# Where four pieces of work stand in a local-attention and mixture-of-experts kernel: slot 0's weights, its table, the first value sums, the query reorders

## The chip, the core and the metric

The kernel runs on one NeuronCore of a Trainium2 chip, as one launch. The metric is the device time of one execution in microseconds (us), lower is better. TensorE is PE in the profile (its weight loads PEld), VectorE DVE, ScalarE ACT, GpSimd POOL, SyncE SP. All loads of inputs and weights are issued from SP's queue in an order that the program fixes; POOL issues the stores of intermediate rows, the gathers and the scatters.

## The reference

The inputs are q, k, v of shape (4, 8, 768, 64): 4 batches, 8 heads, 768 positions, head size 64. Attention is local (a key counts where its position is less than 16 away) plus 24 summary keys per head, one for each block of 32 positions. The result, 3072 tokens of 512 numbers, goes through a mixture of 8 experts, one expert for each token.

```python
k_sum = k.reshape(B, H, nb, 32, D).max(axis=3)
v_sum = v.reshape(B, H, nb, 32, D).mean(axis=3)
scores_l = where(|pos_q - pos_k| < 16, q @ k.T / 8, -1e9)
scores_s = q @ k_sum.T / 8 + log(32)
a = softmax(concat([scores_l, scores_s]))
x = a @ concat([v, v_sum])                      # as (3072, 512)
logits = x @ w_gate;  e = argmax(logits, axis=1)
weight = softmax(logits)[e] * sigmoid(x @ w_output_gate)[e]
out = weight * (relu(x @ w1[e]) @ w2[e])        # w1[e]: 512 x 1024, w2[e]: 1024 x 512
```

## The kernel before

**Attention.** `attention` walks over 48 stages: 4 batches (b), 6 tiles of 128 tokens in each (tok), 2 halves of 4 heads (g). A stage is `scores` (PE multiplies queries `qt` with keys `kt` into `sp`; DVE adds the mask and takes the row's minimum into `sm`, `mn`; ACT takes the exponential into `pr`), `turn_p` (PE transposes `pr` into `pt`, copied to `pT`) and `values` (PE multiplies `pT` with the values `vw` into `pv`; DVE divides by the sum into `xs`). In names of buffers the digits are batch, tile, half: `sm301` is batch 3, tile 0, half 1. `todo` and `second` hang smaller work onto the stages: gate logits, routing, the preparation of the next keys and queries.

**Queries and keys.** Three loads per batch, u = 0 to 2, bring 256 positions each into `raw_q` and `raw_k`. `reorder` copies them into `nat_q` and `nat_k`, mostly on DVE; `prep_q` and `prep_k` transpose those on PE into `qt` and `kt`. `prep_k` also takes the maxima `km` on DVE, and `k_sum` copies `km` into `kt` (four copies, one for each pair of heads). The query load of two u ahead is issued at the first tile of a u, and its reorder stands right behind the load in the program:

```python
            if n2 and tt == 0:
                load("q", q, *n2)
                reorder("q", *n2, RE[5])
```

**Value sums.** `load_vm` brings the values of four heads into `vm` (o = 0 and 1), `v_sum` adds up each block of 32, `mean` divides and stores into the DRAM buffer `vs_dr`, and `load_vsum` brings that into the `vw` tiles. In batch 0 both sums are on DVE (`tensor_reduce`, two halves each); in later batches GpSimd adds them in five halving steps (96x1024, 512, 256, 128, 64).

**The experts.** After two batches the router's counts give a table of three early slots of 256 tokens (`early_slots`, at the event "routed", after stage 36: batch 3, tile 0). `Experts.start` then hangs slot 0's work onto the tiles of batch 3 (`late_work[tok]`): `fetch_list` (which tokens), `fetch` (gathers their rows into `xg`), and `fetch_w` for 12 weight pieces of 256 KB, three on each of the tiles 1 to 4. Every piece is a load on SP into `raw` (6 buffers), a rounding on ACT (`w1h`, `w2h`) and a remainder on DVE (`w1l`, `w2l`). `fetch_w` first has SP read the slot's expert number from the table. `Experts.early` and the slots behind it run once attention has ended.

**What sets the order.** SP's order is that of the program. On PE, DVE, ACT and (in attention) POOL a scheduler that works with modelled times sets the order when the program is built, starting from the order in which the program names the work; on the chip each engine then runs its list strictly in order.

Of the kernel before, what the change touches and what calls it, by code (L numbers as in the profile page):

```python
# [14 lines left out]
AF = mybir.ActivationFunctionType  # L15
ALU = mybir.AluOpType
AX = mybir.AxisListType
# [4 lines left out]
P = 128  # L22
HP = H // 2
NB = S // 64
# [78 lines left out]
def body(tc, q, k, v, w_gate, w_ogate, w1, w2, ident, cst, out):  # L103
    nc = tc.nc
    with (
        tc.tile_pool(name="const", bufs=1, side="left") as const,
        tc.tile_pool(name="ps", bufs=2, space=PSUM) as ps,
        tc.tile_pool(name="dr", bufs=1, space=DRAM) as dr,
        tc.tile_pool(name="tail", bufs=1, side="right") as st,
    ):  # L110
        id_sb = const.tile([P, P], F32, name="id_sb")
        nc.sync.dma_start(id_sb, ident)
        c_sb = const.tile([P, C_END], F32, name="c_sb")
        nc.gpsimd.dma_start(c_sb, cst)
        wg_sb = const.tile([P, NC, 32], F32, name="wg_sb")
        nc.gpsimd.memset(wg_sb, 0.0)
        nc.gpsimd.dma_start(wg_sb[:, :, 0:E], w_gate.rearrange("(c p) e -> p c e", p=P))
        nc.gpsimd.dma_start(wg_sb[:, :, E:2 * E], w_ogate.rearrange("(c p) e -> p c e", p=P))
        x_dr = dr.tile([N, DM], F32, name="x_dr")
        l_dr = dr.tile([E * N + P, 2], I32, name="l_dr")  # L120

        pool_a = tc.tile_pool(name="early", bufs=1, side="left")
        pool_b = tc.tile_pool(name="late", bufs=1, side="right")
        sa, sb = pool_a.__enter__(), pool_b.__enter__()
        rt = route_setup(tc, const, sa, ps, c_sb, l_dr)
        moe = Experts(tc, const, ps, w1, w2, id_sb, x_dr, l_dr, rt, out)
        late_work = [[] for _ in range(TB)]
        with tc.manual_schedule(engines={mybir.EngineType.SP}):
            for event in attention(tc, const, sa, sb, st, ps, dr, q, k, v, id_sb, c_sb, wg_sb, x_dr, l_dr, rt, late_work):
                if event == "last batch":  # L130
                    pool_a.__exit__(None, None, None)
                    moe.open_first(tc.tile_pool(name="moe1", bufs=2, side="left", reuse_waits="tile"))
                elif event == "routed":
                    moe.add_slots(early_slots(tc, const, c_sb, rt))
                    moe.start(late_work)
                elif event[0] == "tiles done":
                    with tc.manual_schedule(engines={mybir.EngineType.Pool}):
                        moe.early(event[1])
        pool_b.__exit__(None, None, None)
        moe.open_second(tc.tile_pool(name="moe2", bufs=2, side="right", reuse_waits="tile"))  # L140
        with tc.manual_schedule(engines={mybir.EngineType.Pool}):
            with tc.manual_schedule(engines={mybir.EngineType.DVE}):
                moe.fetch_w(2, ("e", 0), range(NF // 2, NF))
                moe.fetch_w(1, ("e", 1), range(NF // 2))
            moe.fetch_w(1, ("e", 1), range(NF // 2, NF))
            moe.second(("e", 0), 2, *moe.hidden0, ("e", 1), ("e", 2), 2, 2)
            counts = rest_slots(tc, const, c_sb, rt, moe)
            moe.run()
        moe.rest(counts)
        moe.close()  # L150
# [27 lines left out]
def attention(tc, const, sa, sb, st, ps, dr, q, k, v, id_sb, c_sb, wg_sb, x_dr, l_dr, rt, late_work):  # L178
# [53 lines left out]

    def v_sum(b, o, half):
        t = vm[b, o]
        if b == 0:
            if half == 0:
                vs[b, o] = sb.tile([96, D], F32, name=f"vs{b}{o}", tag="vs", bufs=2)
            hs = slice(32 * half, 32 * half + 32)
            nc.vector.tensor_reduce(out=vs[b, o][:, hs], in_=t.rearrange("p (s d) -> p d s", d=D)[:, hs, :], axis=AX.X, op=ALU.add)
            if half == 1:  # L240
                mean(b, o, vs[b, o])
            return

        n = 16 * D
        if half == 0:
            nc.gpsimd.tensor_tensor(t[:, 0:n], t[:, 0:n], t[:, n:2 * n], ALU.add)
            return
        while n > D:
            n //= 2
            nc.gpsimd.tensor_tensor(t[:, 0:n], t[:, 0:n], t[:, n:2 * n], ALU.add)  # L250
        mean(b, o, t[:, 0:D])

    def mean(b, o, total):
        r2 = sb.tile([96, D], F32, name=f"vm2{b}{o}", tag="vs2", bufs=2)
        nc.vector.tensor_scalar(r2, total, 1.0 / 32.0, None, ALU.mult)
        nc.gpsimd.dma_start(vs_dr[b, 4 * o:4 * o + 4].rearrange("g n d -> (g n) d"), r2)

    def load_vw(b, tok):
# [42 lines left out]
    def k_sum(b):  # L301
        kt = KT[b % 2]
        for hp in range(HP):
            own = kt[:, hp, PAD:PAD + NB * KW].rearrange("p (i w) -> p i w", w=KW)[:, :, 32:56]
            nc.vector.tensor_copy(own, km[b, 0][:, hp, :].unsqueeze(1).to_broadcast([P, NB, NS]))  # L305

    def prep_q(b, u, gs=(0, 1)):
        qt = QT[(3 * b + u) % 2]
# [204 lines left out]
    for i, (b, tok, g) in enumerate(stages):  # L513
        u, tt = tok // 2, tok % 2
        n1, n2 = step_after(b, u), step_after(b, u, 2)
        more = b + 1 < B
        if (b, tok, g) == (B - 1, 0, 0):
            yield "last batch"
        if g == 0:
            if n2 and tt == 0:  # L520
                load("q", q, *n2)
                reorder("q", *n2, RE[5])
            load_ahead(*((b + 1, tok) if tok < 4 else (b + 2, tok - 6)))
            if more and tok in (0, 1, 3):
                reorder("k", b + 1, (tok + 1) // 2, RE[6])
            if (tok + 2 < TB or more) and (b, tok) != (0, 0):
                nb, ntok = divmod(b * TB + tok + 2, TB)
                load_vw(nb, ntok)
                load_vsum(nb, ntok)
        first, second = todo.pop(i, []), []  # L530
        s = 2 * tt + g
        if n1 and s == 0:
            first.append(lambda: prep_q(*n1, gs=(0,)))
        if n1 and s == 1:
            second.append(lambda: prep_q(*n1, gs=(1,)))
        if more and s == 0:
            second.append(lambda: prep_k(b + 1, u, (0,)))
        if more and s == 2:
            second.append(lambda: prep_k(b + 1, u, (1,)))
            if u == 2:  # L540
                second.append(lambda: k_sum(b + 1))
        if more and u < 2 and s in (1, 3):
            second.append(lambda: v_sum(b + 1, u, s // 2))
        if b == B - 1:
            w = late_work[tok]
            take = w[:-(-len(w) // 2)] if g == 0 else w[:]
            del w[:len(take)]
            second += take
        if i + 1 < n:
            scores(i + 1)  # L550
        for work in first[:1]:
            work()
        turn_p(i)
        second = first[1:] + second
        for work in second:
            work()
        if i > 0:
            values(i - 1)
            pb, ptok, pg = stages[i - 1]
            if pg == 1:  # L560
                todo.setdefault(i + 1, []).append(lambda pb=pb, ptok=ptok: turn_x(pb, ptok))
                if ptok % 2 == 1:
                    todo.setdefault(i + 2, []).append(lambda pb=pb, ptok=ptok: logits(pb, ptok))
                    todo.setdefault(i + 4, []).append(lambda pb=pb, ptok=ptok: turn_logits(pb, ptok))
                if ptok == TB - 1:
                    todo.setdefault(i + 4, []).append(lambda pb=pb: route_to(pb))
                    todo.setdefault(i + 6, []).append(lambda pb=pb: route_to(pb))
        if i == n - 2 * TB:
            yield "routed"
    for i in sorted(todo):  # L570
        for work in todo[i]:
# [154 lines left out]
class Experts:  # L726
# [38 lines left out]
    def fetch_list(self, s, n):  # L765

        nc, tc = self.tc.nc, self.tc
        nm = f"lst_{s[0]}{s[1]}"
        lst = self.const.tile([P, 2, 2], I32, name=nm, tag=nm)
        for t in range(n):  # L770
            i = nc.gpsimd.indirect_dma_start(out=lst[:, t, :], out_offset=None, in_=self.l_dr,
                                             in_offset=bass.IndirectOffsetOnAxis(ap=self.slots[s][0][t], axis=0))
# [82 lines left out]

    def start(self, late_work):

        self.fetch_list(("e", 0), 2)
        late_work[1] += [lambda: self.fetch(("e", 0), 2)]
        late_work[3] += [lambda: self.fetch_list(("e", 1), 2)]  # L860
        parts = [(1, i) for i in range(NF)] + [(2, i) for i in range(NF // 2)]
        for x, (which, i) in enumerate(parts):
            late_work[1 + x * 4 // len(parts)].append(lambda which=which, i=i: self.fetch_w(which, ("e", 0), [i]))

    def early(self, route):

# [180 lines left out]
```

## Time and profile before

| | |
|---|---|
| median of 3 runs | 545.28 us (544.25, 545.28, 550.03) |
| profiled execution | 543.33 us, of which the span from the first to the last instruction is 541.5 us |
| PE busy | 494.3 us (91%), mean granted clock 0.964 |
| DVE busy | 395.6 us (73%) |
| ACT busy | 336.9 us (62%) |
| POOL busy | 200.0 us (37%) |
| moved by DMA | 117.98 MB, mean 218 GB/s |

Times in the profile count from the span's start. A row of the timeline gives start, length, engine, line, operation and tiles, and in brackets how long the engine stood idle before it and what ended that. SPq and POOLq rows are DMA issues, whose length is the issue and not the transfer. A line number belongs to the kernel before.

### The profile page before, as it was taken

The page shows a single profiled execution, that of the slowest core. Times are in us where ns is not written, and L with a number is a line of the kernel's source. Part 1 is how long each engine was busy: PE and PEld are TensorE (multiplying, and loading weights), DVE is VectorE, ACT ScalarE, POOL GpSimd, SP SyncE. Part 2 cuts the span into 40 slices and gives each one's busy share as a digit, 9 for nine tenths or more (in the row PEclk, how much of TensorE's full clock was granted, in tenths as well). Part 3 has the DMA queues.
Part 4 walks back from the last instruction along what each step waited for, and adds up shares of the span by engine and source line. Part 5 has one row for each costly group of instructions (what it writes and reads, how often), then busy time and mean ns, then how long its engine had stood idle before and what let it go on. Part 6 is the DMA issues. An engine that isn't in the chain of part 4 may idle for free.

```text
span 541.5 us, 12266 instructions
## 1 busy us (share of the span) xinstructions
PE 494.3 (91%) x3880; PEld 431.7 (80%) x3880; DVE 395.6 (73%) x1242; ACT 336.9 (62%) x752; POOL 200.0 (37%) x225
## 2 busy tenths in 40 slices
PE   6499998989878899999999999999999999999990
PEld 6497787777767688899898988989897887886970
DVE  7979798769938878989657657665767866767770
ACT  4487786586748957465556546555556756658560
POOL 7037155545451252343734160511332421511421
PEclk7699998999979999999999999999999999999995
DMA  8979899899783757695947658495576795597641
GB/s 247 236 199 269 212 233 282 158 201 235 169 202 79 264 172 235 238 240 129 351 160 264 204 206 291 142 307 172 202 248 218 271 334 193 208 324 235 207 149 30
DMA packets 117052, 117.98 MB, mean 218 GB/s; under 512 B 53787, under 2 KB 78651, under 8 KB 116192
## 3 DMA queue, kind: packets, MB, share of 16 engines
q1 hardware_dynamic: 107584, 97.02, 63.2%
q0 software_dynamic: 9376, 19.91, 11.6%
q8 instruction: 36, 0.59, 0.5%
q14 instruction: 56, 0.46, 0.3%
HBM read 106.30 MB, written 13.79 MB: 222 GB/s over the span
## 4 chain that ended last, share of the span: by engine, by line
PE 66%; DMA 12%; DVE 7%; ACT 5%; issue 5%; POOL 2%; SPq 1%; POOLq 0%; ACTq 0%; DVEq 0%
PE yp L935 8%; PE hp L836 8%; PE hp L835 8%; PE yp L933 8%; PE yp L934 8%; PE hp L837 8%; PE sp L330 6%; DMA xg<-x_dr,lst_w 5%; DMA raw_q<-in_q_dram 3%; PE pv L359 3%; PE pt L348 2%; PE xp L817 2%; ACT pr L340 2%; DMA vm<-in_v_dram 2%; ACT qt L201 1%
## 5 line engine op out<-in xcount | busy, mean ns | idle before, releaser
L836 PE MATMUL hp<-xhl,w1h 128*128 128x256 f32 x384 | 108.8, 284 | 0.3 <-issue 0.3
L835 PE MATMUL hp<-xhl,w1h 128*128 128x256 f32 x384 | 108.5, 284 | 0.3 <-PE yp L935 0.3
L837 PE MATMUL hp<-xhl,w1l 128*128 128x256 f32 x384 | 108.5, 283 | 0.0
L933 PE MATMUL yp<-w2h,hh 128*128 128x512 f32 x216 | 86.7, 401 | 1.3 <-ACT hh L904 1.2
L935 PE MATMUL yp<-w2h,hl 128*128 128x512 f32 x216 | 85.0, 396 | 0.2
L934 PE MATMUL yp<-w2l,hh 128*128 128x512 f32 x216 | 84.9, 393 | 0.0
L340 ACT ACTIVATE pr<-sm,mn 128x120 f32<-128x120 f32 x192 | 62.0, 387 | 23.5 <-DVE mn L338 22.5
L784 POOL DMA_INDIRECT xg<-x_dr,lst_w x26 | 30.2, 1162 | 125.2 <-PE xp L817 120.2
L835 PEld LDWEIGHTS hp<-xhl,w1h 128*128 128x128 f32 x384 | 73.2, 191 | 2.4 <-issue 1.2
L836 PEld LDWEIGHTS hp<-xhl,w1h 128*128 128x128 f32 x384 | 73.5, 191 | 2.0 <-issue 1.0
L837 PEld LDWEIGHTS hp<-xhl,w1l 128*128 128x128 f32 x384 | 73.5, 191 | 0.0
L838 ACT ACTIVATE hh<-hp 128x256 fp32r<-128x256 f32 x96 | 35.3, 380 | 52.8 <-PE hp L837 43.8
L839 DVE SCALAR_TENSOR_TENSOR hl<-hp,hh 128x256 fp32r<-128x256 f32 x96 | 39.0, 420 | 39.3 <-ACT hh L838 25.3
L330 PE MATMUL sp<-kt,qt 128*128 128x120 f32 x384 | 57.7, 298 | 7.0 <-DVE kt L305 6.0
L330 PEld LDWEIGHTS sp<-kt,qt 128*128 128x128 f32 x384 | 52.7, 211 | 10.0 <-issue 7.7
L338 DVE CUSTOM_DVE_ANT_0 sm<-sp,c_sb 128x120 f32<-128x120 f32 x192 | 42.9, 276 | 15.1 <-PE sp L330 9.3
L933 PEld LDWEIGHTS yp<-w2h,hh 128*128 128x128 f32 x216 | 40.7, 188 | 10.2 <-ACT hh L904 2.1
L935 PEld LDWEIGHTS yp<-w2h,hl 128*128 128x128 f32 x216 | 40.4, 188 | 9.7 <-DVE hl L905 1.2
L934 PEld LDWEIGHTS yp<-w2l,hh 128*128 128x128 f32 x216 | 40.7, 188 | 7.8
L348 PE MATMUL pt<-id_sb,pr 128*120 128x128 f32 x192 | 38.9, 290 | 2.9 <-ACT pr L340 2.9
L359 PE MATMUL pv<-vw,pT 120*64 120x65 f32 x768 | 34.9, 228 | 3.3 <-DMA raw_('e', 0)_6_2972<-in_moe_w_dram 1.6
L359 PEld LDWEIGHTS pv<-vw,pT 120*64 120x64 f32 x768 | 27.8, 137 | 11.7 <-issue 3.9
(735 smaller groups left out, 1043.4 us busy)
## 6 DMA issues: line engine op xcount, KB each, us to landing
vw<-in_v_dram SPq DMA_DIRECT2D x88, 96.0 KB
raw_k<-in_k_dram SPq DMA_DIRECT2D x12, 512.0 KB
raw_q<-in_q_dram SPq DMA_DIRECT2D x12, 512.0 KB
vm<-in_v_dram SPq DMA_DIRECT2D x8, 768.0 KB
x_dr<-xs POOLq DMA_DIRECT2D x24, 256.0 KB
vw<-vs_dr SPq DMA_DIRECT2D x36, 48.0 KB
vw<-in_v_dram SPq DMA_DIRECT2D x8, 64.0 KB
xg<-x_dr,lst_w POOLq DMA_INDIRECT x26
```

The costliest lines, as they stand in the source:

```text
L330: nc.tensor.matmul(sp[:, 2 * x + y, 0:W], lhsT=qt[:, 2 * g + x, li, :], rhs=kt[:, 2 * g + x, blk * KW:blk * KW + W], start=True, stop=True)
L338: nc.vector.tensor_tensor_reduce(out=sm[:, c, :], in0=sp[:, c, 0:W], in1=c_sb[:, m:m + W], scale=1.0, scalar=3.0e38, op0=ALU.add, op1=ALU. ...
L340: nc.scalar.activation(pr[:, c, :], sm[:, c, :], AF.Exp, bias=mn[:, c:c + 1], scale=-1.0)
L348: nc.tensor.transpose(pt[:, c, :], pr[:, c, :], id_sb)
L359: nc.tensor.matmul(po[64 * y:64 * y + 64, 2 * x + hh, :], lhsT=pT[:, 2 * x + y, 64 * hh:64 * hh + 64], rhs=VW[(NB * b + 2 * tok + y) % VR] ...
L835: nc.tensor.matmul(hp, lhsT=w_h[:, fs], rhs=self.xh[:, c, :], start=c == 0, stop=False)
L836: nc.tensor.matmul(hp, lhsT=w_h[:, fs], rhs=self.xl[:, c, :], start=False, stop=False)
L837: nc.tensor.matmul(hp, lhsT=w_l[:, fs], rhs=self.xh[:, c, :], start=False, stop=c == NC - 1)
L839: nc.vector.scalar_tensor_tensor(hl[:, j, :], hp, 0.0, hh[:, j, :].bitcast(F32), ALU.max, ALU.subtract)
L933: nc.tensor.matmul(y, lhsT=hh[:, j, tk], rhs=w_h, start=j == 0, stop=False)
L934: nc.tensor.matmul(y, lhsT=hh[:, j, tk], rhs=w_l, start=False, stop=False)
L935: nc.tensor.matmul(y, lhsT=hl[:, j, tk], rhs=w_h, start=False, stop=j == NF - 1)
```

## The change

Five edits. (1) `Experts.start` is called at "last batch", before stage 36, and its lists move: the weight pieces to tiles 0 to 3, three each; slot 0's list to tile 1 and its gather to tile 2. (2) The event "routed", with the early slots' table, comes after stage 33 (batch 2, tile 4). (3) In batch 0 the sum o = 1 takes the GpSimd way of the later batches and its mean is a GpSimd instruction; the sum o = 0 stays on DVE, but may not be scheduled ahead of the last `k_sum` copy, and its mean goes to ACT. (4) The query reorder stands at the second tile of a u, one tile behind its load. (5) An assertion that the scatters of the first two batches exist.

```diff
@@ body
                 if event == "last batch":
...
+                    moe.start(late_work)
                 elif event == "routed":
                     moe.add_slots(early_slots(tc, const, c_sb, rt))
-                    moe.start(late_work)
@@ v_sum
-        if b == 0:
+        if (b, o) == (0, 0):
...
-            nc.vector.tensor_reduce(out=vs[b, o][:, hs], ...)
+            i = nc.vector.tensor_reduce(out=vs[b, o][:, hs], ...)
+            tc.add_manual_dep(i.ins, km["last"].name, ... NoSync, SCHED_ONLY)
@@ mean
-        nc.vector.tensor_scalar(r2, total, 1.0 / 32.0, None, ALU.mult)
+        if b == 0 and o == 0:
+            nc.scalar.activation(r2, total, AF.Copy, scale=1.0 / 32.0)
+        else:
+            (nc.gpsimd if b == 0 else nc.vector).tensor_scalar(r2, total, 1.0 / 32.0, None, ALU.mult)
@@ attention, at the first half of a tile
             if n2 and tt == 0:
                 load("q", q, *n2)
+            elif n2:
                 reorder("q", *n2, RE[5])
@@ attention, at the end of a stage
-        if i == n - 2 * TB:
+        if i == n - 2 * TB - 3:
             yield "routed"
@@ Experts.start
-        self.fetch_list(("e", 0), 2)
-        late_work[1] += [lambda: self.fetch(("e", 0), 2)]
+        late_work[1] += [lambda: self.fetch_list(("e", 0), 2)]
+        late_work[2] += [lambda: self.fetch(("e", 0), 2)]
         late_work[3] += [lambda: self.fetch_list(("e", 1), 2)]
...
-            late_work[1 + x * 4 // len(parts)].append(... fetch_w(which, ("e", 0), [i]))
+            late_work[x * 4 // len(parts)].append(... fetch_w(which, ("e", 0), [i]))
```

How the rows move on the engines, at the places that the prediction speaks of:

DVE at the start of batch 0, before: `vs_276` and `vs_282` are the sums o = 0 and 1, `vm_187` and `vm_189` the values they read, `km` the key maxima, `kt` the keys, `sm_309` the first stage's scores.

```order
L296 TENSOR_REDUCE km_200<-ktr_230 128x2x8
L239 TENSOR_REDUCE vs_276<-vm_187 96x32 x2
L305 COPY kt_143<-km_200 128x12x24
L296 TENSOR_REDUCE km_200<-ktr_238 128x2x8
L305 COPY kt_143<-km_200 128x12x24
L239 TENSOR_REDUCE vs_282<-vm_189 96x32 x2
L255 TENSOR_SCALAR vm_279<-vs_276 96x64
L305 COPY kt_143<-km_200 128x12x24 x2
L338 ISA sm_309,mn_310<-sp_304,c_sb 128x120
```

The same place with the change:

```order
L303 TENSOR_REDUCE km_200<-ktr_230 128x2x8
L312 COPY kt_143<-km_200 128x12x24
L303 TENSOR_REDUCE km_200<-ktr_238 128x2x8
L312 COPY kt_143<-km_200 128x12x24 x3
L239 TENSOR_REDUCE vs_276<-vm_187 96x32 x2
L346 ISA sm_311,mn_312<-sp_306,c_sb 128x120
```

The maxima and all key copies now precede a single pair of value sums, and the first scores follow that pair; the second pair is gone from DVE.

DVE at the border of batches 2 and 3, before, with numbers: `nat_q32` is the last query reorder, `xs25` the end of batch 2, `sm300` the first scores of batch 3.

```order
L368 RECIPROCAL den25_2459<-den25_2459 128x4
L220 COPY nat_q32_2499<-raw_q32_2497 128x1024
L369 TENSOR_TENSOR xs25_2458<-pv251_2541,den25_2459 128x256
L197 COPY ls23_2379<-lp23_2374 128x256
L338 ISA sm300_2424,mn300_2425<-sp300_2419,c_sb_68 128x120
```

The same place with the change; only the first of the four `sm300` rows is shown in both:

```order
L377 TENSOR_TENSOR xs25_2503<-pv251_2601,den25_2504 128x256
L346 ISA sm300_2469,mn300_2470<-sp300_2464,c_sb_68 128x120
...
L303 TENSOR_REDUCE km3_1770<-ktr321_2433 128x2x8
L312 COPY kt1_148<-km3_1770 128x12x24 x2
L220 COPY nat_q32_2668<-raw_q32_2542 128x1024
L197 COPY lg2_2259<-lt23_2566 128x32
L346 ISA sm301_2555,mn301_2556<-sp301_2550,c_sb_68 128x120
```

The reorder has moved behind `xs25`, `ls23`, the whole of `sm300`, the last maxima and two key copies.

SP in batch 3 with the change, with numbers: `vw4` to `vw7` are the value tiles of tiles 2 and 3, `esia` the table with the expert numbers, `raw1_('e', 0)` the first weight pieces.

```order
L278 DMA vw5_166<-vs_dr_178 24x8x64
L804 TENSOR_LOAD esia_2376
...
L813 DMA raw1_('e', 0)_0_2593<-in_moe_w1_dram 128x512
...
L813 DMA raw1_('e', 0)_1_2597<-in_moe_w1_dram 128x512
...
L813 DMA raw1_('e', 0)_2_2650<-in_moe_w1_dram 128x512
L271 DMA vw6_169<-in_v_dram 48x8x64
```

Before, the loads of `vw6` and `vw7` stood at the place of the table's read and the three pieces, and these came one tile's loads later.

More of the change, by code (lines that the diff above doesn't have):

```diff
@@ L238, in v_sum @@
             hs = slice(32 * half, 32 * half + 32)
-            nc.vector.tensor_reduce(out=vs[b, o][:, hs], in_=t.rearrange("p (s d) -> p d s", d=D)[:, hs, :], axis=AX.X, op=ALU.add)
+            i = nc.vector.tensor_reduce(out=vs[b, o][:, hs], in_=t.rearrange("p (s d) -> p d s", d=D)[:, hs, :], axis=AX.X,
+                                        op=ALU.add)
+            tc.add_manual_dep(i.ins, km["last"].name, mybir.DependencyInfo(mybir.DependencyClass.NoSync,
+                                                                           mybir.DependencyReason.SCHED_ONLY))
             if half == 1:
@@ L304, in k_sum @@
             own = kt[:, hp, PAD:PAD + NB * KW].rearrange("p (i w) -> p i w", w=KW)[:, :, 32:56]
-            nc.vector.tensor_copy(own, km[b, 0][:, hp, :].unsqueeze(1).to_broadcast([P, NB, NS]))
+            i = nc.vector.tensor_copy(own, km[b, 0][:, hp, :].unsqueeze(1).to_broadcast([P, NB, NS]))
+        km["last"] = i.ins
     def prep_q(b, u, gs=(0, 1)):
@@ L769, in fetch_list @@
         lst = self.const.tile([P, 2, 2], I32, name=nm, tag=nm)
+        assert s[0] != "e" or len(self.rt["scatters"]) >= FIRST * TB
         for t in range(n):
@@ L862, in start @@
         for x, (which, i) in enumerate(parts):
-            late_work[1 + x * 4 // len(parts)].append(lambda which=which, i=i: self.fetch_w(which, ("e", 0), [i]))
+            late_work[x * 4 // len(parts)].append(lambda which=which, i=i: self.fetch_w(which, ("e", 0), [i]))
     def early(self, route):
```

## The prediction

> **What bounds the kernel now.** I read busy time by stretches first. Each row: the stretch in us, its length, busy time of PE, PEld, DVE, ACT and POOL (instructions in brackets), PE's granted clock, the DMA engines' share, GB/s.
>
> ```profile
> 0.00:24.00 24.00, 12.90 (x85) 11.88 (x86) 20.30 (x30) 9.49 (x19) 10.05 (x35) 0.73 1.01 250
> 24.00:140.00 116.00, 106.90 (x1204) 91.52 (x1205) 95.46 (x483) 84.53 (x228) 54.27 (x62) 0.97 1.02 223
> 140.00:192.00 52.00, 43.27 (x485) 36.83 (x485) 38.98 (x225) 39.32 (x103) 17.87 (x22) 0.93 0.64 169
> 192.00:488.00 296.00, 293.42 (x1896) 260.05 (x1895) 210.73 (x460) 176.78 (x352) 105.45 (x97) 1.00 0.70 233
> 488.00:541.50 53.50, 37.77 (x217) 31.41 (x216) 30.14 (x51) 26.77 (x51) 12.32 (x11) 0.89 0.48 156
> ```
>
> From 192 us to 488 us PE stands still for 2.6 us of 296: the experts are PE's own time. The chain that ended last shows their beat in the transposes of a slot's tokens, 23.49 us apart:
>
> ```profile
> 265.48 0.87 PE xp L817 x8
> 288.96 0.87 PE xp L817 x8
> ```
>
> The change removes no matmul and adds none, so the experts' 350 us can only start earlier. What it can win lies ahead of 192 us, where PE is idle for 11.1 + 9.1 + 8.7 = 28.9 us, and that only where PE's idle time has a cause that the change touches. There no single engine is full: from 24 to 140 us PE is busy 92%, DVE 82%, ACT 73%, and the DMA share is 1.02. Waits in this part are shared out among four resources, so a stall that goes is not always kept.
>
> **Edit 3, the first sums.** Rows of the timeline at the start, DVE first:
>
> ```profile
> 15.06 3.66 DVE L239 TENSOR_REDUCE vs<-vm 96x32 f32<-96x1024 f32 x2 [0.65 <-DMA vm<-in_v_dram]
> 18.64 0.30 DVE L305 COPY kt<-km 128x288 f32<-128x288 f32 x1
> 18.86 0.68 DVE L296 TENSOR_REDUCE km<-ktr 128x16 f32<-128x512 f32 x1
> 19.68 3.64 DVE L239 TENSOR_REDUCE vs<-vm 96x32 f32<-96x1024 f32 x2
> 23.77 0.27 DVE L338 CUSTOM_DVE_ANT_0 sm<-sp,c_sb 128x120 f32<-128x120 f32 x1
> 14.53 0.66 ACT L201 ACTIVATE kt<-ktr 128x256 f32<-128x256 f32 x2
> 24.09 1.25 ACT L340 ACTIVATE pr<-sm,mn 128x120 f32<-128x120 f32 x4 [6.28 <-DVE mn L338]
> 25.66 0.52 POOL L256 DMA_DIRECT2D vs_dr<-vm  x1 [1.40 <-DVE vm L255]
> 28.51 1.61 SPq L271 DMA_DIRECT2D vw<-vs_dr  x4
> 32.47 0.45 PE L359 MATMUL pv<-vw,pT 120*64 120x65 f32 x4
> ```
>
> DVE spends 3.66 + 3.64 = 7.3 us on sums before the first scores at 23.77, and ACT stands idle 6.28 us for them. With the change the last maximum waits only for ACT's key copies (done at 15.19): 0.68 us and three key copies of 0.30 follow, so the remaining pair of sums starts at about 16.8 and ends at 20.4. The first scores come at 20.4 instead of 23.77: 3.3 us earlier.
>
> The values do not follow by as much, since `vw` needs both sums through `vs_dr`. On POOL the second sum now costs five adds; their means are in the groups of the later batches (count | busy us, mean ns of one | idle before):
>
> ```profile
> L246 POOL TENSOR_TENSOR vm<-vm 96x1024 f32<-96x1024 f32 x6 | 14.2, 2363 | 18.7 <-DMA vm<-in_v_dram 18.7
> L250 POOL TENSOR_TENSOR vm<-vm 96x512 f32<-96x512 f32 x6 | 8.3, 1384 | 0.3
> L250 POOL TENSOR_TENSOR vm<-vm 96x256 f32<-96x256 f32 x6 | 4.8, 804 | 0.3
> L250 POOL TENSOR_TENSOR vm<-vm 96x64 f32<-96x64 f32 x6 | 3.2, 538 | 0.3
> L250 POOL TENSOR_TENSOR vm<-vm 96x128 f32<-96x128 f32 x6 | 2.7, 457 | 0.3
> ```
>
> 2.36 + 1.38 + 0.80 + 0.46 + 0.54 = 5.5 us. The trace has no mean on POOL; it lies between nothing and the 0.54 of the add of the same width, and I take 0.54. With one store issue of 0.52 between, 6.6 us. When `vm` for o = 1 has landed isn't shown: after 15.06 (the one before it) and by 19.68 (DVE did not wait for it). So the second store is issued between 21.7 and 26.3, against 25.66 now: the values move by -4.0 to +0.6 us, middle -1.7. ACT's mean is a small operation in its idle 6.28 us and costs nothing; without that cover it would delay the exponentials by less than the 0.66 of its key copies. Scores ahead by 3.3, values by 1.7: I take **-2.5 us**, ends +0.6 and -4.0.
>
> The skill speaks against this edit. The Trainium skill, "SBUF — State Buffer", section "Who interferes with whom", says that a DVE copy in a two-port mode and a GpSimd instruction exclude each other, the later one waiting out the whole instruction. In this trace a router operation that meets a POOL add looks like that; the last row is the same operation, undisturbed, in the stretch from 120 to 140 us (0.20 us):
>
> ```profile
> 81.80 2.36 POOL L246 TENSOR_TENSOR vm<-vm 96x1024 f32<-96x1024 f32 x1 [4.64 <-DMA vm<-in_v_dram]
> 82.75 1.48 DVE L422 TENSOR_TENSOR oh<-c_sb,first 128x48 f32<-128x48 f32 x1
> L422 DVE TENSOR_TENSOR oh<-c_sb,first 128x48 f32<-128x48 f32 x1 | 0.2, 196 | 0.0
> ```
>
> The key copies at 16 us would be such copies: if the 2.36 us add is in front of them, the first scores come at up to 22.8 and this term is near zero. I keep -2.5, since the add can't start before its values land, and price the collisions as a rival.
>
> **Edit 4, the reorders.** The row of the waits (us in total, times, longest), then DVE at the two large ones, with the query's load on SP, PE's gap and PE's clock behind it:
>
> ```profile
> DVE nat_q L220 <- DMA raw_q<-in_q_dram: 5.3, 4, 3.1
> 116.81 0.69 DVE L220 COPY nat_q<-raw_q 128x1024 f32<-128x1024 f32 x1 [1.47 <-DMA raw_q<-in_q_dram]
> 144.78 0.40 SPq L209 DMA_DIRECT2D raw_q<-in_q_dram  x1
> 152.89 0.69 DVE L220 COPY nat_q<-raw_q 128x1024 f32<-128x1024 f32 x1 [3.11 <-DMA raw_q<-in_q_dram]
> 154.30 0.94 PE L379 MATMUL xtr<-id_sb,xs 128*128 128x128 f32 x4 [2.78 <-DVE ls L197]
> 156.00:160.00 4.00, 4.00 (x19) 3.89 (x20) 1.06 (x4) 2.14 (x5) 2.54 (x3) 0.50 0.86 245
> ```
>
> DVE waits four times for a query that is still under way, 5.3 us in all. The wait at 152.89 holds up the first scores of batch 3 behind it in DVE's list, PE idles 2.78 us, and its clock in the next slice is 0.50. DVE ran out of work at 152.89 - 3.11 = 149.78. The order shows the reorder behind those scores, `xs25`, `ls23`, a maximum and two key copies: by the durations above (4 x 0.27, 0.68, 2 x 0.30, and about 0.4 each for the other two) 3.2 us of work, after which 152.9 has come. The reorder at 116.81 moves back by a whole stage's scores in the same way. Waits of 1.47 + 3.11 = 4.6 us go; what is late next is the second half's scores, which need keys that ACT copies. I take **-4.6**, ends 0 (the next instruction waits as long for something else) and -8.0 (all 5.3, and the halved clock of 156 to 160 us too, which is worth 2.0, and 0.7 for the rest). The loads keep their place on SP.
>
> On the clock: the Trainium skill, "TensorE: Matmul & The Clock Gate", section "What's actually happening", gives about 3.4 us of idling as what halves the clock. Here the gap was 2.78 us and the clock was 0.50 all the same, so the trace asks for less; by the rule a gap cut to 1 us would leave the clock whole, which is the -8.0 end.
>
> **Edits 1 and 2, slot 0's weights and table.**
>
> ```profile
> 157.61 0.39 SPq L803 DMA_DIRECT2D raw_('e', 0)_0_2701<-in_moe_w_dram  x1
> 172.25 0.31 SPq L264 DMA_DIRECT2D vw<-in_v_dram  x1
> 179.28 0.63 ACT L805 ACTIVATE w1h<-raw_('e', 0)_3_2823 128x512 fp32r<-128x512 f32 x1 [0.66 <-DMA raw_('e', 0)_3_2823<-in_moe_w_dram]
> 181.14 0.63 ACT L805 ACTIVATE w1h<-raw_('e', 0)_5_2880 128x512 fp32r<-128x512 f32 x1 [0.23 <-DMA raw_('e', 0)_5_2880<-in_moe_w_dram]
> 184.14 0.63 ACT L805 ACTIVATE w1h<-raw_('e', 0)_6_2972 128x512 fp32r<-128x512 f32 x1 [0.17 <-DMA raw_('e', 0)_6_2972<-in_moe_w_dram]
> 182.69 0.76 PE L359 MATMUL pv<-vw,pT 120*64 120x65 f32 x16 [1.59 <-DMA raw_('e', 0)_6_2972<-in_moe_w_dram]
> ```
>
> SP stands still before 172.25, since the next value load needs a `vw` tile that PE still uses; pieces 3 to 5 queue behind it and reach ACT late (0.66 + 0.23 + 0.17 = 1.06 us idle), PE loses 1.59. With the change pieces 3 to 5 take the place of 0 to 2, ahead of that wait, and land some 10 us before ACT needs them; pieces 6 to 8 then follow 172.25 but are asked for later. I take **-1.0**, ends -1.6 and +1.0 (three pieces of 256 KB now precede the loads of `vw6` and `vw7`: 0.77 MB at the 245 GB/s of that slice is 3.1 us, for tiles that are read two tiles later). SP's read of the table gains no wait as the table keeps its place in DVE's list. Slot 0's list and gather keep their places in POOL's list: nothing. The end of attention still decides when the experts begin: their first transposes use PSUM buffers of the scores.
>
> **The sum.** -2.5 - 4.6 - 1.0 = -8.1 us if all is kept. Where the loads run at a share of 1.02, compute that comes 3 us sooner meets them sooner; I hand back a fifth, which is my choice: **-6.5**. The profiled execution of 543.33 (span 541.5 and 1.8 around it) becomes 536.8. The median of the runs lies 1.95 above that execution, so I predict 538.8.
>
> **Rivals.**
> - *Nothing kept* (0.18). The loads bound the part up to 140 us, so the start is given back, and behind the removed query wait the key reorder of the same load time waits. For it: the share 1.02 over 116 us. Against it: no DVE wait for `raw_k` shows among the large ones. Only the weights' -1.0 stays: 544.3.
> - *The reorder still waits* (0.10): the scheduler moved it by its modelled times, and one stage is not a tile. Then -2.5 - 1.0 stay: 541.8.
> - *All kept, and the clock too* (0.14): -8.1 - 2.7 = -10.8, 534.5.
> - *Slower through GpSimd's adds* (0.12). Seven sums of five adds instead of six, at other places beside DVE. A collision costs 1.48 - 0.20 = 1.3 us of DVE. Five more of them eat the -6.5; ten more make it +6.5, 551.8. It decides if the router's operations and copies of each batch fall under the adds, which only the run can tell.
>
> **How the numbers follow.** The forecast has 0.46, from -9 to -4 us, that is 536 to 541. A measurement here tells about 1% (5.4 us) from no change. Faster by more than that: two thirds of the forecast (0.32) and the third rival (0.14), 0.46. Within 1%: the rest of the forecast (0.14), both first rivals (0.28), a quarter of the last (0.03), 0.45. Slower by more: 0.09. The range 531 to 548 leaves out half of the third rival's lower side and the last one's upper part, some 0.15.
>
> **What would show it.** Right: first scores near 20.4 us and the first `pv` near 30.8; no DVE wait above 1 us for `raw_q`; the clock slice behind 152 us at 1.00; no ACT wait for pieces 3 to 6; the transposes of slot 0's tokens 6 us earlier than in the row below, and the slots' beat of 23.49 kept. Wrong: key copies of more than 1 us around 16 us, stretched router operations in number, or a new DVE wait for `raw_k` in place of `raw_q`.
>
> ```profile
> 191.87 0.60 PE L817 MATMUL xp<-id_sb,xg 128*128 128x128 f32 x4
> ```

## The result and the profile after

The change takes **538.58 us** (median of 4 runs, 537.39 to 539.6) against 545.93 us for the kernel before beside it: the medians lie 7.4 us apart, and the ratio is 0.989 with a 95% interval of 0.984 to 0.994, which is -6.2 us (-8.9 to -3.5). Measured a second time, on another chip, the ratio was 0.992 (0.989 to 0.995), -4.4 us (-6.2 to -2.5). 538.8 had been predicted. The total was met, but not by the working behind it: the largest of its three terms stands for an edit that moved nothing on any engine.

The profiled execution took 537.39 us, with a span of 535.6 us. Busy time by stretches, in the columns used before (stretch, length, PE, PEld, DVE, ACT, POOL, clock, DMA share, GB/s):

```profile
0.00:24.00 24.00, 17.31 (x121) 15.49 (x121) 21.10 (x50) 13.01 (x32) 15.18 (x39) 0.86 1.01 251
24.00:140.00 116.00, 104.69 (x1184) 88.62 (x1183) 89.95 (x478) 83.81 (x229) 53.27 (x63) 0.97 0.99 223
140.00:192.00 52.00, 45.32 (x540) 37.36 (x538) 40.45 (x221) 39.77 (x99) 21.95 (x27) 1.00 0.71 172
192.00:488.00 296.00, 293.68 (x1850) 259.71 (x1849) 210.22 (x450) 177.95 (x354) 103.83 (x96) 1.00 0.71 235
```

The gain is in the first and the third row. PE does 4.4 us more before 24 us (17.31 for 12.90) and 2.1 us more from 140 to 192 us. In the long stretch between them it does 2.2 us **less** (104.69 for 106.90), so that at 140 us half of the lead is left. The chain that ended last shows the slots' beat as it was, 283.79 - 260.30 = 23.49 us, and both transposes 5.2 us earlier than the rows at 265.48 and 288.96:

```profile
260.30 0.87 PE xp L827 x8
283.79 0.87 PE xp L827 x8
```

The start, in the timeline. Compare the first scores with 23.77, the second store of sums with 25.66 and the first `pv` with 32.47:

```profile
15.29 0.74 DVE L312 COPY kt<-km 128x288 f32<-128x288 f32 x3
15.95 3.70 DVE L239 TENSOR_REDUCE vs<-vm 96x32 f32<-96x1024 f32 x2
18.42 2.36 POOL L250 TENSOR_TENSOR vm<-vm 96x1024 f32<-96x1024 f32 x1 [7.52 <-DMA vm<-in_v_dram]
19.57 0.27 DVE L346 CUSTOM_DVE_ANT_0 sm<-sp,c_sb 128x120 f32<-128x120 f32 x1
24.73 0.39 POOL L262 TENSOR_SCALAR vm<-vm 96x64 f32<-96x64 f32 x1
25.42 0.57 POOL L263 DMA_DIRECT2D vs_dr<-vm  x1 [0.30 <-POOL vm L262]
31.46 0.45 PE L367 MATMUL pv<-vw,pT 120*64 120x65 f32 x4
```

The scores come 4.2 us sooner, the values 1.0: the second sum on GpSimd can't begin before its values land at 18.4, and its store goes out at 25.42, where it was 25.66. The list of DVE's waits (us in total, times, longest) tells of the query reorders:

```profile
DVE nat_q L220 <- DMA raw_q<-in_q_dram: 13.0, 7, 3.6
DVE nat_k L220 <- DMA raw_k<-in_k_dram: 3.0, 3, 1.4
```

These waits were to go. They are 13.0 us in 7 instead of 5.3 us in 4, and new ones for keys, 3.0 us in 3, stand beside them.

### The profile page after: what moved, and what is told of

It is laid out like the page before. It is cut to its first block, busy times and chain, and to the rows that moved or that the text cites. A ratio compares the mean times of both kernels' runs of the same rounds, so it can differ in the third digit from the quotient of the medians.

```text
span 535.6 us, 12274 instructions
## 1 busy us (share of the span) xinstructions
PE 492.9 (92%) x3880; PEld 428.5 (80%) x3880; DVE 387.0 (72%) x1238; ACT 336.2 (63%) x753; POOL 204.1 (38%) x231
## 4 chain that ended last, share of the span: by engine, by line
PE 61%; DMA 17%; DVE 6%; SPq 5%; issue 4%; ACT 3%; POOL 0%; POOLq 0%; ACTq 0%; DVEq 0%
PE hp L846 8%; PE hp L845 8%; PE hp L847 8%; PE yp L945 7%; PE yp L943 7%; PE yp L944 7%; DMA xg<-x_dr,lst_w 5%; PE sp L338 4%; DMA raw_q<-in_q_dram 4%; DMA vw<-vs_dr 3%; PE pv L367 3%; DMA raw_k<-in_k_dram 2%; PE pt L356 2%; PE xp L827 2%; SPq L272 1%
## 5 line engine op out<-in xcount | busy, mean ns | idle before, releaser
L338 PE MATMUL sp<-kt,qt 128*128 128x120 f32 x384 | 53.6, 287 | 2.2 <-DVE mn L346 0.8
L338 PEld LDWEIGHTS sp<-kt,qt 128*128 128x128 f32 x384 | 48.4, 199 | 5.6 <-issue 2.3
L367 PE MATMUL pv<-vw,pT 120*64 120x65 f32 x768 | 36.3, 231 | 6.8 <-DVE xs L377 2.8
```

What stands on the lines that cost most here:

```text
L338: nc.tensor.matmul(sp[:, 2 * x + y, 0:W], lhsT=qt[:, 2 * g + x, li, :], rhs=kt[:, 2 * g + x, blk * KW:blk * KW + W], start=True, stop=True)
L367: nc.tensor.matmul(po[64 * y:64 * y + 64, 2 * x + hh, :], lhsT=pT[:, 2 * x + y, 64 * hh:64 * hh + 64], rhs=VW[(NB * b + 2 * tok + y) % VR] ...
```

## The experiments

All ratios are to the kernel before on the same chip, with 95% intervals; the chips differ (medians of before from 538.7 to 545.6 us), so kernels of different groups are compared by ratio alone. Gains in us are the ratio's share of 545.9, and the times in the expectations are meant at that level. Two things hold for all of them. The scheduler sets the lists (the orders of the operations) of PE, DVE, ACT and POOL anew for every kernel, so a kernel can differ from its neighbour far from the line that was edited. And where two kernels have the same lists, nothing is seen through which the edit could act.

**First group: each edit alone.** The kernel before with edit 3 (`v_sum`, `mean`, `k_sum` as in the change):

```diff
-        if b == 0:
+        if (b, o) == (0, 0):
...
+            tc.add_manual_dep(i.ins, km["last"].name, ...)
...
+        if b == 0 and o == 0:
+            nc.scalar.activation(r2, total, AF.Copy, scale=1.0 / 32.0)
```

> The kernel before with edit 3 alone (first value sums behind the key copies, second sum on GpSimd). Sum of terms: the start's 2.5 us is kept on the way to the experts: 541 to 543.5 us, about 2.5 under before, and the query waits stay at about 5 us. Loads bind: the scores start 4 us sooner, the query waits behind them grow by 3 us or more, and nothing or less than 1 us is kept: 545 to 546.

Measured: 0.9915 (0.988 to 0.995), -4.6 us (-6.8 to -2.5). DVE's waits in this kernel:

```profile
DVE nat_q L220 <- DMA raw_q<-in_q_dram: 14.2, 5, 5.1
```

Each theory has half: the query waits grow by 9 us, as "loads bind" said, and a gain is kept all the same. Edit 3 alone also moves the query reorders. At the border of batches 2 and 3 the reorder already stands behind the first scores, the last maximum and two key copies:

```profile
152.87 0.53 DVE L312 COPY kt<-km 128x288 f32<-128x288 f32 x2
156.86 0.69 DVE L220 COPY nat_q<-raw_q 128x1024 f32<-128x1024 f32 x1 [3.46 <-DMA raw_q<-in_q_dram]
```

With edit 4 alone:

```diff
             if n2 and tt == 0:
                 load("q", q, *n2)
+            elif n2:
                 reorder("q", *n2, RE[5])
```

> The kernel before with edit 4 alone (queries reordered a tile behind their load). Sum of terms: the waits of 1.47 and 3.11 us go, 541 to 542 us, about 4.6 under before, DVE waits for queries under 1 us in all. Loads bind: DVE waits for queries as long as before or longer, the time is within 2 us of before unless the work that stands ahead of the wait now keeps PE from stopping; then PE's gap of 2.78 us behind 154 us is what shrinks and the granted clock of that slice is whole.

Measured: 0.997 (0.994 to 1.000), -1.5 us (-3.1 to 0). DVE waits 8.7 us for queries in 3 waits, the longest 5.1. The term of -4.6 lies outside the interval. At the border the reorder stands where it stood before, ahead of `xs` and the first scores:

```profile
153.41 0.69 DVE L220 COPY nat_q<-raw_q 128x1024 f32<-128x1024 f32 x1 [5.05 <-DMA raw_q<-in_q_dram]
154.02 0.42 DVE L369 TENSOR_TENSOR xs<-pv,den 128x256 f32<-128x256 f32 x1
154.68 0.27 DVE L338 CUSTOM_DVE_ANT_0 sm<-sp,c_sb 128x120 f32<-128x120 f32 x1
```

It is so everywhere. The traces of this kernel and of before have the same operations in the same order on PE (3880 matmuls), DVE, POOL and SP, and on ACT too but for one weight rounding behind 420 us that is one place off, as one also is between two traces of the change. Edit 4 moves a call in the program, and the scheduler makes the same lists of it. So the -1.5 us are no gain of edit 4: they show how far apart two kernels with the same lists were measured here, and so do the 5.3 and 8.7 us of query waits.

With edits 1 and 2 alone:

```diff
+                    moe.start(late_work)
...
-        if i == n - 2 * TB:
+        if i == n - 2 * TB - 3:
...
-            late_work[1 + x * 4 // len(parts)].append(...)
+            late_work[x * 4 // len(parts)].append(...)
```

> The kernel before with edits 1 and 2 alone (slot 0's weights from tile 0 on, its table in batch 2). Sum of terms: 1.0 us under before, 544 to 546, ACT's waits for pieces 3 to 6 gone. Rival, the queue of loads: the pieces are issued in 20 us in which the DMA engines were busy 28 to 55 percent, so that the traffic at 176 to 184 us is gone and 3 us or more are kept: 541 to 543.

Measured: 0.9985 (0.995 to 1.002), -0.8 us (-2.6 to +0.9). ACT's waits for pieces 3 to 6 are gone; one of 1.38 us for a later piece is new. Edit 3 alone and this kernel add up to -5.4 us. The whole measured -6.2 and -4.4, so a loss in combining them can be neither shown nor excluded.

The change with edit 4 taken back (the diff of edit 4, reversed):

> The changed kernel with edit 4 taken back (queries reordered right behind their load again). Sum of terms: without the 4.6 us, 542 to 544. Loads bind and the query's place in DVE's list is all: near before, 544 to 546, with DVE waiting for queries 10 us or more. If the edits 1 to 3 carry the gain: 538 to 540.

Measured: 0.995 (0.991 to 0.998), -2.9 us (-4.7 to -1.1) or 543.0, in the first band, but not for the band's reason. This kernel has the lists of the change, to the same exception on ACT, so it is a third measurement of the change. The three intervals share the stretch from -4.7 to -3.5 us. What a single execution's waits say is as loose: at the border these lists give a query wait of 2.73 us in the change's first trace, none in its second and 4.67 us here, at 154.85.

**Second group: edit 3 taken back, and the loads.** The change again, and the change without edit 3:

> The changed kernel itself, for its ratio beside the runs that follow. Both theories: 1.1 percent under before, as measured. If the singles add up, 1.3 percent.

> The changed kernel with edit 3 taken back (the sums on DVE ahead of the first scores). Sum of terms as predicted: 2.5 us more than the change (0.5 percent). From the runs of the single edits: edit 3 carries two thirds of the gain, so this one keeps 0.3 to 0.45 percent, 2 us under before and 3 to 5 us more than the change.

Measured: 0.992 (0.989 to 0.995) and 0.998 (0.995 to 1.002). Edit 3 is worth 0.6% or 3.4 us on top of the others, 4.6 alone; that is most of the gain either way. The second kernel has the lists of edits 1 and 2 alone, which it measures once more, at -0.9 us (-2.8 to +1.0). Its query waits are 2.5 us, and those of edit 3 alone 14.2: the faster kernel waits longer, so these waits are not the price that the prediction took them for.

Then the question what the query waits hang on. The change with each query load a tile earlier:

```diff
-            if n2 and tt == 0:
-                load("q", q, *n2)
-            elif n2:
-                reorder("q", *n2, RE[5])
+            if (b, tok) == (0, 0):
+                load("q", q, *n2)
+            if tt == 1:
+                if step_after(b, u, 3):
+                    load("q", q, *step_after(b, u, 3))
+                if n2:
+                    reorder("q", *n2, RE[5])
```

> The changed kernel with each query's load issued a tile earlier, in the same two buffers; the bytes are the same. If the place of the load in SP's queue is what DVE waits for: the query waits fall from 13 us to under 4, and the time is 2 to 5 us under the change. If the DMA engines' share is the limit: the query waits go, waits for keys, values and sums of the same size come in their place, and the time is within 1.5 us of the change.

Measured: 1.000 (0.996 to 1.004), 4.5 us **slower** than the change. The second theory had the exchange of waits but not its price. The query waits fall from 11.9 us (the change on this chip) to 4.7, but SP's own waits and GpSimd's, in this kernel:

```profile
SPq L278 <- DMA vs_dr<-vm: 16.8, 4, 8.2
POOL vm L250 <- DMA vm<-in_v_dram: 34.8, 6, 8.2
```

In the change on that chip these rows read 6.6 and 24.9:

```profile
SPq L278 <- DMA vs_dr<-vm: 6.6, 2, 3.7
POOL vm L250 <- DMA vm<-in_v_dram: 24.9, 6, 9.5
```

The queries were brought forward at the cost of the values: GpSimd waits longer for them, and SP, which issues in the order of the program, stands longer at the sums' read-back. The waits were exchanged, not removed. The lists of DVE and PE differ too from 42 us on, and what of the 4.5 us is due to that isn't shown.

The change with more to move:

```diff
             load_ahead(*((b + 1, tok) if tok < 4 else (b + 2, tok - 6)))
+            if b < 3:
+                spare = dr.tile([P // 2, H, 2 * D], F32, name=f"spare{b}{tok}")
+                nc.sync.dma_start(spare, k[b, :, P * tok:P * (tok + 1), :].rearrange(...))
```

> The changed kernel with one more transfer of 256 KB in each of the first 18 tiles (a copy that nothing reads). If the attention part hangs on the loads: 18 x 256 KB are 4.7 MB, at the 223 to 250 GB/s of that part 19 to 21 us, and the time rises by 15 to 20 us. If the loads have room and only their order counts: it rises by less than 5 us. In between, the share kept says how much of that part is load time.

Measured: 1.0025 (0.999 to 1.006), 1.06% or 5.8 us over the change (3 to 8 by the two intervals) for 19 to 21 us of transfers: about three tenths. The stretch from 24 to 140 us, of this kernel and of the change on the same chip:

```profile
24.00:140.00 116.00, 106.05 (x1195) 89.73 (x1193) 91.68 (x473) 84.32 (x229) 53.70 (x61) 0.98 1.04 243
24.00:140.00 116.00, 103.27 (x1177) 87.08 (x1176) 90.03 (x475) 83.16 (x228) 53.23 (x64) 0.98 0.99 222
```

The DMA engines moved 243 GB/s where they had moved 222 at a "full" share of 0.99. So a share of 0.99 did not mean that nothing more went through. Two limits: the added copy goes from DRAM to DRAM and not into a tile, and the lists of DVE and PE differ from 46 us on. The query waits are 0.8 us here, with 3.5 us more before one reorder for which the profile names no cause, against 11.9 in the change, although more was moved.

**Third group: which half of edit 3.** The change with the order only, all sums and means on DVE behind the key copies:

```diff
-        if (b, o) == (0, 0):
+        if b == 0:
...
-            (nc.gpsimd if b == 0 else nc.vector).tensor_scalar(r2, ...)
+        nc.vector.tensor_scalar(r2, total, 1.0 / 32.0, None, ALU.mult)
```

> The changed kernel with the order of edit 3 alone: all four half sums and both means on DVE, behind the key copies, nothing on GpSimd. If the offload to GpSimd carries edit 3: the two sums of 3.7 us still stand ahead of the first scores, these come at 23.3 us or so, and the time is that of the change without edit 3, 0.0 to 0.4 percent under before. If the order carries it: first scores near 20 us, 0.8 to 1.2 percent under before.

Measured: 1.008 (1.003 to 1.012). The first scores come at 23.61, as the offload's theory said, but the time is above both bands. One part shows in the chain of the profiled execution: the second beat of the slots is 292.09 - 266.43 = 25.66 us, 2.2 over 23.49. Why, and what makes up the rest, stays open.

```profile
23.61 0.27 DVE L343 CUSTOM_DVE_ANT_0 sm<-sp,c_sb 128x120 f32<-128x120 f32 x1
266.43 0.98 PE xp L824 x7
292.09 0.87 PE xp L824 x8
```

The change with the offload only (the scheduler free to put the remaining sum ahead of the key copies):

```diff
-            tc.add_manual_dep(i.ins, km["last"].name, ...)
```

> The changed kernel with the offload of edit 3 alone: the second sum on GpSimd, the first mean on ScalarE, but the first sum where DVE had it, ahead of the last maxima and key copies. If the offload carries edit 3: first scores at 19.5 to 20.5 us and 0.8 to 1.2 percent under before, as the change. If the order carries it: 0.0 to 0.4 percent under before.

Measured: 1.002 (0.999 to 1.005): the offload alone is worth nothing. Its timeline shows why:

```profile
18.38 2.34 POOL L248 TENSOR_TENSOR vm<-vm 96x1024 f32<-96x1024 f32 x1 [7.50 <-DMA vm<-in_v_dram]
18.90 1.98 DVE L310 COPY kt<-km 128x288 f32<-128x288 f32 x1
21.41 2.28 DVE L310 COPY kt<-km 128x288 f32<-128x288 f32 x3
23.98 0.28 DVE L344 CUSTOM_DVE_ANT_0 sm<-sp,c_sb 128x120 f32<-128x120 f32 x1 [0.29 <-PE sp L336]
```

The key copies now fall under GpSimd's adds: one takes 1.98 us instead of 0.3, three take 2.28 instead of 0.74, and the first scores come at 23.98, where they were before. So the early first scores need both halves of edit 3: without the offload two sums stand ahead of the scores, and without the order the copies collide with GpSimd. Neither half alone is faster than before, though the lists of both kernels also differ from the change's throughout attention. The Trainium skill, "SBUF — State Buffer", section "Who interferes with whom", describes this exclusion between a two-port DVE copy and a GpSimd instruction; the 1.98 us agree, since the copy ends at 20.88 and the add that began before it at 20.72.

The last two runs try for a version faster than the change. GpSimd adds the piece of values that lands first, DVE the other, behind the first four score operations:

```diff
-        if (b, o) == (0, 0):
+        if (b, o) == (0, 1):
...
-        if b == 0 and o == 0:
+        if b == 0 and o == 1:
...
+    scores(0)
+    for o, half in todo_sums:
+        v_sum(0, o, half)
...
+        if i == 0:
+            km["last"] = last.ins
```

> The changed kernel with the two sums exchanged: GpSimd adds the first piece of values, which lands near 15 us, DVE reduces the second, which lands between 18 and 20 us, and does so behind the four maxima of the first scores. First scores at 17.0 to 17.5 us instead of 19.6, the second store of sums issued at 23 instead of 25.4, the first value products near 29 instead of 31.5. If the start is kept on the way to the experts: another 2 to 2.5 us under the change, 1.2 to 1.6 percent under before. If the loads take it back: the query waits grow by as much and the time is within 1 us of the change.

Measured: 0.998 (0.994 to 1.002). The piece lands before the key copies, so they collide again, and the first scores come at 19.26 (only this kernel's start is read here):

```profile
15.32 2.34 POOL L250 TENSOR_TENSOR vm<-vm 96x1024 f32<-96x1024 f32 x1 [4.44 <-DMA vm<-in_v_dram]
15.82 3.52 DVE L312 COPY kt<-km 128x288 f32<-128x288 f32 x3
```

So GpSimd was held until they are done:

```diff
+        if (b, o, half) == (0, 0, 0):
+            i = nc.vector.tensor_copy(t[:, 0:1], t[:, 0:1])
+            tc.add_manual_dep(i.ins, km["keys"].name, ...)
```

> The kernel with the exchanged sums, and GpSimd's first add held until DVE's key copies are done (DVE touches one column of the first piece of values behind them). If the key copies of 3.52 us in the run before were stretched by GpSimd's add: they fall to 0.74 us as in the change, the first scores come near 17 us instead of 19.3, the second store of sums is issued near 22.5, and with the start kept the time is 1.2 to 1.6 percent under before; if something later takes the start back, the copies are short all the same and the time is 0.2 to 1.0 percent under before. If GpSimd is not what stretches them: they stay above 2 us.

Measured: 1.0005 (0.997 to 1.004). The copies are short again (0.74), which shows that GpSimd stretched them. But the time is that of before:

```profile
15.83 0.74 DVE L316 COPY kt<-km 128x288 f32<-128x288 f32 x3
16.71 2.35 POOL L254 TENSOR_TENSOR vm<-vm 96x1024 f32<-96x1024 f32 x1 [5.83 <-DVE vm L250]
18.25 0.28 DVE L351 CUSTOM_DVE_ANT_0 sm<-sp,c_sb 128x120 f32<-128x120 f32 x1 [1.63 <-PE sp L343]
19.07 3.73 DVE L239 TENSOR_REDUCE vs<-vm 96x32 f32<-96x1024 f32 x2
22.73 0.27 DVE L351 CUSTOM_DVE_ANT_0 sm<-sp,c_sb 128x120 f32<-128x120 f32 x1
25.05 0.24 ACT L264 ACTIVATE vm<-vs 96x64 f32<-96x64 f32 x1
25.59 0.52 POOL L267 DMA_DIRECT2D vs_dr<-vm  x1 [2.08 <-ACT pr L353]
```

Four score operations come at 18.25, but the next four only at 22.73, behind the sum, where the change has its first eight done by 21.3. And the sum, done at 22.8, waits for ACT until 25.05, behind the exponentials, so its store is no earlier than in the change. That may be why nothing is gained, but it isn't shown: PE has done 16.84 us of work before 24 us here, against 17.31 and 15.84 in the two traces of the change, so it starts as early and loses the lead later, with DVE's and PE's lists differing from the change's from the start on. No version under the change was found.

## Why the prediction was right, and where it was not

**Edit 3: the order at the start was right, the worth of the lead is not explained.** Predicted -2.5 (ends +0.6 and -4.0); measured -4.6 alone (-6.8 to -2.5) and -3.4 on top of the others, so the term is at the low end of what was measured. The first scores were put at 20.4 and came at 19.57, since the sums started at 15.95, not 16.8. The values were put at -1.7 and moved -0.24 at the store, -1.0 at the first `pv`; the range was right, the middle was not (GpSimd's mean took 0.39 of the 0.54). The condition in the text, that this term is near zero when the add stands in front of the key copies, is what the offload alone showed: 23.98, with 22.8 at most foreseen. That edit 3 carries the gain is shown: the four measurements with edit 3 whole and the loads as they were (-4.6, -6.2, -4.4, -2.9) all lie clear of no change, and the three without it (-1.5, -0.8, -0.9) have intervals that reach it. How it does so is not. The reading at hand is the lead on PE, 17.31 us of work before 24 us instead of 12.90. But the exchanged sums with GpSimd held had 16.84 and no gain, so the lead alone is not enough. The rival, that the lists edit 3 makes of the rest of attention carry part of it, was not tested.

**Edit 4: the term of -4.6 stood for nothing.** The step that failed is "the order shows the reorder behind those scores", taken as the work of edit 4. The order shown ahead of the prediction is that of all edits together. Edit 4 alone leaves every list as it was; edit 3, as a side effect on the scheduler, moves the reorder. And when it is moved, the waits of 1.47 + 3.11 don't go: all query waits, 5.3 us before, become 13.0. The step took the landing of the load as fixed at 152.9. In the change DVE reached the reorder at 152.26, near the 153.0 that follows from the prediction's 149.78 and 3.2, but the load landed 2.1 us later, though it was issued only 0.2 us later:

```profile
145.00 0.83 SPq L209 DMA_DIRECT2D raw_q<-in_q_dram  x1
154.99 0.69 DVE L220 COPY nat_q<-raw_q 128x1024 f32<-128x1024 f32 x1 [2.73 <-DMA raw_q<-in_q_dram]
155.84 0.66 PE L387 MATMUL xtr<-id_sb,xs 128*128 128x128 f32 x4 [1.28 <-DVE lg L197]
156.00:160.00 4.00, 4.00 (x47) 3.19 (x47) 2.17 (x17) 3.82 (x11) 2.19 (x3) 1.00 0.92 226
```

PE's gap is 1.28 instead of 2.78 us there, and the clock of the next slice is whole, where it had been 0.50. That is no sure gain either: the same lists gave 0.60 for this slice in the kernel with edit 4 taken back. At 100.53 the other thing happens: DVE comes to a reorder 3.0 us sooner than before (96.92 for 99.95), the load lands no sooner, and DVE waits 3.61 us, with the next `pv` behind it:

```profile
100.53 0.69 DVE L220 COPY nat_q<-raw_q 128x1024 f32<-128x1024 f32 x1 [3.61 <-DMA raw_q<-in_q_dram]
102.28 1.14 PE L367 MATMUL pv<-vw,pT 120*64 120x65 f32 x16 [2.80 <-DVE xs L377]
```

**Edits 1 and 2: the mechanism was right, the time is too small to tell.** Predicted -1.0, measured -0.8 (-2.6 to +0.9) and -0.9 (-2.8 to +1.0). Of ACT's waits for pieces 3 to 6 only one is left, 0.41 for piece 6, which is issued at 168.79 behind `vw6` and `vw7` as foreseen:

```profile
173.68 0.63 ACT L815 ACTIVATE w1h<-raw_('e', 0)_6_2837 128x512 fp32r<-128x512 f32 x1 [0.41 <-DMA raw_('e', 0)_6_2837<-in_moe_w_dram]
```

**The sum.** -8.1 less a fifth was -6.5; measured -6.2 and -4.4, and -2.9 with edit 4 taken back and the same lists. That 538.8 was met is luck. Without the term of edit 4 the same working gives -2.5 - 1.0 = -3.5, less a fifth -2.8. Edit 3 measured 1 to 2 us more than its term, which made up for part of the term that stood for nothing. The fifth handed back for a DMA share of 1.02 was a guess, and no run measures it: the extra loads price more bytes, not earlier compute.

**The signs named.** First scores near 20.4: yes, 19.57. First `pv` near 30.8: no, 31.46. No DVE wait above 1 us for `raw_q`: no, the longest is 3.6. The clock behind 152 us at 1.00: yes in this trace, 0.60 in another with the same lists. No ACT wait for pieces 3 to 6: all but 0.41. Slot 0's transposes 6 us earlier: yes, 185.71 for 191.87. The beat kept: yes. Of the signs against it, the waits for `raw_k` did appear, 3.0 us, and the gain was there all the same.

```profile
185.71 0.49 PE L827 MATMUL xp<-id_sb,xg 128*128 128x128 f32 x3
```

**The rivals.** "Nothing kept" is refuted: its -1.0 lies outside all three intervals of these lists. Its mechanism, the loads as the next limit, fits the longer query waits from 24 to 140 us, but isn't shown to cost anything. "The reorder still waits" came nearest for edit 4: it named the scheduler, which left the edit without effect, and its -3.5 for the whole lies among the measurements. "Slower through GpSimd's adds" did not come about: two router operations take over 1 us, where there were three (1.48, 1.48 and 1.70). Its collision is real, and at the key copies it takes the early scores away, unless the order puts them out of reach.

```profile
82.59 1.47 DVE L459 TENSOR_SCALAR eo<-eo 128x6 f32<-128x6 f32 x1
125.73 2.13 DVE L430 TENSOR_TENSOR oh<-c_sb,first 128x48 f32<-128x48 f32 x1
```

## What to carry to other kernels

Where a scheduler sets the lists, look at the list of each engine with one edit alone before crediting that edit: here one edit changed no list, and another moved what the first was credited with. The length of the waits for a load is not what they cost: edit 3 alone has 14.2 us of query waits and is faster than the change without it, which has 2.5. Moving an operation from DVE to GpSimd took both the offload and a place in time in which DVE had no copies to run beside it; either alone was worth nothing here. And among loads that share one queue, ask first what stands behind the one that you bring forward: here it was the values, and the kernel lost 4.5 us.

## What was not expected of the hardware

A DMA share of 0.99 left room: with extra transfers the same stretch moved 243 GB/s instead of 222, and only about three tenths of their time was paid.

The clock fell behind short gaps of PE, but not behind all of them. Behind the gap of 1.28 us in the change it was 1.00. Around and after the gap of 2.80 us at 102.28 it was 0.78 and 0.80, and the `pv` in that row takes 1.14 us for 16 products that take 0.69 at 96 us. In the kernel before, it was 0.71 in the slice behind a gap of 1.71 us at 87.45, and 1.00 in the one behind a gap of 1.62 us at 119.97, so the length of one gap does not tell.

```profile
96.00 0.69 PE L367 MATMUL pv<-vw,pT 120*64 120x65 f32 x16
100.00:104.00 4.00, 1.72 (x24) 1.15 (x24) 2.36 (x6) 0.70 (x2) 1.18 (x2) 0.78 0.69 151
104.00:108.00 4.00, 3.75 (x26) 2.97 (x23) 3.71 (x19) 1.55 (x5) 2.10 (x3) 0.80 0.88 219
```

And from the kernel before:

```profile
87.45 0.63 PE L282 MATMUL qtr<-id_sb,nat_q 128*128 128x128 f32 x4 [1.71 <-DVE den L368]
88.00:92.00 4.00, 3.57 (x41) 3.43 (x41) 3.67 (x26) 2.59 (x7) 1.43 (x3) 0.71 1.15 245
119.97 0.65 PE L282 MATMUL ktr<-id_sb,nat_k 128*128 128x128 f32 x4 [1.62 <-ACT qt L201]
120.00:124.00 4.00, 4.00 (x50) 3.59 (x52) 3.50 (x21) 3.98 (x14) 0.00 (x0) 1.00 1.08 222
```

The Trainium skill, "TensorE: Matmul & The Clock Gate", section "What's actually happening", puts the idling that lowers the clock at about 3.4 us; the traces of the change and of before show it lowered behind 2.80, 2.78 and 1.71.
